# A new order of steps: sums ahead of a hold on GpSimd's queue, and transposes, loads and sums at other places

## The chip, the cores and the metric

The kernel runs on one core of a Trainium2 chip. The time is device time in microseconds (us) of that core. The engines have their own instruction streams and run them in order: TensorE (PE, matmuls and their weight loads), VectorE (DVE), ScalarE (ACT), GpSimd (POOL) and SyncE (SP). DMA transfers are issued from the streams of POOL, SP and ACT. An instruction that waits for a semaphore stops everything behind it in its own stream.

## The reference

Two layers follow each other. The first is an attention without softmax, 8 batches, 8 heads, 576 positions, head size 64:

```
kv  = einsum('bhsd,bhse->bhde', k, v)
out = einsum('bhsd,bhde->bhse', q, kv)
rms = sqrt(mean(out * out, axis=-1, keepdims=True) + 1e-06)
out = out / rms * g_norm
```

Its output, with the heads side by side, is x of shape (8, 576, 512) for the second, a gate with a long convolution:

```
proj = x @ w_proj                       # w_proj: (512, 1536)
x1, x2, x3 = thirds of proj, 512 columns each
X2 = rfft(x2, n=576, axis=1);  H = rfft(filter_fft, n=576, axis=0)
x2_conv = irfft(X2 * H, n=576, axis=1)
y = x1 * x2_conv * x3
return y @ w_out                        # w_out: (512, 512)
```

Inputs and outputs are float32. The kernel multiplies in bfloat16.

## The kernel before

All 8 batches go through one pipeline. A batch is cut into steps, each a Python function of a few instructions on one engine (line numbers are the profile's). The whole program is one string of words, `ORDER` (L20 to L55). A word such as `Ga1.0` means step `Ga1` of batch 0; a third number means that so many filler matmuls (L112) are put in front of it. A loop at the end (L782 to L786) reads the words and calls the steps one after the other:

```
    for word in ORDER.split():
        n, b, *idle = word.split(".")
        b, tmp["idle"] = int(b), int(idle[0]) if idle else 0
        clock[0] += 1
        step[n](b)
```

So the order of the words is the order of the instructions on each engine. Semaphores are set by the framework from what each instruction reads and writes; nothing else decides when something runs. PSUM is four double banks (`ps_0` to `ps_3`, shown as ps_66 to ps_69), handed out by `take` and `free` in the order of the words.

The steps of a batch, in the order in which its data goes through them:

- `Lk`, `Lv`, `Lq` (L140, L144; with a or b: half of the heads) load k, v and q from HBM, issued on POOL's queue and converted to bfloat16 on the way. The buffers kb, vb and qb exist twice, one for even and one for odd batches. `Lw1`, `Lw2`, `Lw3` (L152) load the thirds of w_proj, `Lwo` loads w_out, `Lf` the filter.
- q has to be transposed. For batches 0 and 1 TensorE does it (`T0`, `T1`, L416, copied out by `eTa`, `eTv`). For batches 2 to 7 step `Qt` does it: a DMA transpose from qb to qT, issued on SP's queue (L407), and a copy of two elements of the result on GpSimd (L408, `one__101<-qT`). This copy serves no computation. It waits until the transpose has landed, and since POOL's stream is in order, no later load is issued before that. It is called a hold here.
- `K` (L377) multiplies k by v, `eK` copies the result out, `O` (L447) multiplies by q, `sq`, `ob`, `ov`, `R`, `rs`, `x` (L454 to L489) normalise into x.
- `Ga`, `Gb` (L631) are the gate's matmuls with w_proj's first and third part, `x1`, `xv`, `g` (L637, L639) copy out and multiply the two.
- `eo`, `fa`, `fr` (L501 to L512, VectorE) fold x along the positions, `abM`, `abT`, `rrM`, `rrT` (L529 to L549) multiply with w_proj's second part, `eab`, `eT`, `err` copy out.
- `F0`, `F1t`, `F1`, `F2c`, `F2` (L571 to L598) are the forward transform. Its results in PSUM are multiplied by the filter's spectrum: `M0`, `M1` (L606) write four products in float32 to `tpw`, `M2` (L621) writes to Y directly. These are VectorE instructions with one input in PSUM.
- The products of `M0` and `M1` are added pairwise into Y (L612): `A0`, `A1` on GpSimd, or `Av0`, `Av1` on VectorE.
- `Io`, `I` (L661, L662) are the inverse transform from Y, `oa`, `ea` (L665) copy out, `vB`, `w`, `fin`, `f` (L671 to L683, VectorE, all operands in SBUF) put the pieces together and multiply by the gate.
- `U`, `U4`, `V` (L716, L729, L754) multiply with w_out, `ot`, `va`, `vv` copy out, and DMAs on SP's queue (L723, L736), at the end also on POOL's and ACT's, store the rows.

The steps of neighbouring batches are interleaved, so that the inverse transform of a batch stands among the gates of the next and the attention of the one after. TensorE's stream is in order, too: an inverse transform whose Y isn't complete stops every matmul behind it.

Of the kernel before, what the change touches and what calls it, by code (L numbers as in the profile page):

```python
# [19 lines left out]
ORDER = """Lqa.0 Zi.0 Lva.0 Zd.0 Z.0 T0.0.20 Lka.0 Lvb.0 Zt.0 Lkb.0 An.0 Lqb.0 Zf.0 eTa0.0 Tb2.0.5 Ka.0 eKva.0 Tb0.0 O01.0.3  # L20
sq1.0 Tb1.0.1 sq0.0 ov0.0 Kb.0.4 Lf.0 ob1.0 Lq.1 T1.0.2 eTv1.0 R1.0 Act.0 eKab.0 rs1.0 R0.0.3 O23.0 rs0.0 sq2.0 ob2.0
sq3.0 x0.0 Ff0.0 Lw3.0 ov3.0 Ff1.0 Ff2.0 R3.0 T1.1 rs3.0 T0.1 Lw1.0 R2.0 Lw2.0 eo0.0 rs2.0 x1.0 eTv1.1 eTa0.1 H1.0
eo1.0 H0.0 H2.0 fr.0 Lv.1 Ga1.0 Gb0.0 Lk.1 Lka.2 x11.0 Gb1.0 Ga0.0 fa0.0 fa1.0 Lq.2 rrM.0 HN0.0 g1.0 Lkb.2 x10.0 g0.0
rrT.0 K.1 verr.0 eK.1 Ga3.0 HN1.0 xv3.0 O01.1 sq0.1 F0.0 sq1.1 abM.0 ob1.1 abT.0 M0.0 ob0.1 eab.0 O23.1 eT.0 Lv.2
sq3.1 Lwo.0 F2c.0 ob3.1 F2.0 M2.0 Gb3.0 sq2.1 F1t.0 g3.0 F1.0 Lv.3 R3.1 R2.1 Lq.3 ob2.1 rs3.1 Ga2.0 Qt.2 rs2.1 x12.0
R1.1 K.2 A0.0 M1.0 R0.1 Av1.0 rs1.1 eK.2 Gb2.0 rs0.1 Io01.0 g2.0 oa01.0 Io23.0 oa23.0 I01.0 x.1 ea01.0 O01.2 sq0.2
Lk.3 I23.0 ea23.0 Ga2.1 ob0.2 eo.1 x12.1 Lq.4 fa.1 Ga3.1 sq1.2 x13.1 R0.2 rs0.2 ob1.2 abM.1 vB.0 abT.1 R1.2 eab.1 eT.1
fr.1 rrM.1 Lv.4 O23.2 rs1.2 sq2.2 ob2.2 w.0 F2c.1 rrT.1 fin.0 err.1 F2.1 Gb3.1 sq3.2 F0.1 Lka.4 M2.1 K.3 ob3.2 g3.1
F1t.1 R2.2 Qt.3 Lkb.4 eK.3 M0.1 F1.1 Ga1.1 rs2.2 R3.2 x11.1 Gb2.1 Gb1.1 M1.1 rs3.2 g2.1 O23.3 x1.2 g1.1 x0.2 U0.0 A0.1
sq2.3 sq3.3 eo.2 ob3.3 ob2.3 Ga0.1 fa.2 A1.1 ot0.0 I01.1 Io23.1 ea01.1 x10.1 Gb0.1 I23.1 Io01.1 oa23.1 abT.2 ea23.1  # L30
abM.2 fr0.2 g0.1 fr1.2 oa01.1 O01.3 eT.2 eab.2 Ga1.2 sq1.3 Ga0.2 vB.1 x11.2 R3.3 w.1 ov1.3 x10.2 rs3.3 Lqa.5 K.4 sq0.3
F1t.2 F1.2 Qt.4 rrM.2 fin.1 ob0.3 eKm.4 rrT.2 M1.2 F2c.2 Gb1.2 R0.3 err.2 F2.2 g1.2 rs0.3 F0.2 R1.3 M2.2 Gb0.2 R2.3
rs1.3 U2.0 Lq.6 rs2.3 M0.2 g0.2 Av1.2 Lk.5 ot2.0 x1.3 Ga2.2 x12.2 O23.4 sq2.4 Lv.5 U0.1 A0.2 x0.3 sq3.4 ob3.4 Ga3.2
ot0.1 ob2.4 Gb3.2 eo.3 x13.2 fa.3 I01.2 g3.2 U4.1 fr1.3 ea01.2 I23.2 Io23.2 ea23.2 Lqb.5 Io01.2 oa01.2 abT.3 oa23.2
vB01.2 ot4.1 R2.4 abM.3 eT.3 Gb2.2 vB23.2 rs2.4 eab.3 O01.4 F1t.3 F1.3 fr0.3 g2.2 sq0.4 ob0.4 sq1.4 rrM.3 Lka.6 ob1.4
rrT.3 Ga1.3 M1.3 err.3 x11.3 R1.4 rs1.4 Lkb.6 w023.2 R0.4 F0.3 rs0.4 U2.1 A1.3 Qt.5 ot2.1 w001.2 w123.2 R3.4 Ga0.3
F2c.3 w101.2 f001.2 M0.3 rs3.4 K.5 F2.3 xv0.3 M2.3 f101.2 Gb0.3 Gb1.3 eK.5 f023.2 g0.3 A0.3 Ga2.3 I23.3 I01.3 g1.3
x12.3 Io01.3 ea23.3 f123.2 Qt.6 ea01.3 x0.4 Lv.6 x1.4 Ga3.3 oa01.3 Io23.3 eo.4 x13.3 Gb3.3 O23.5 oa23.3 g3.3 U0.2
sq3.5 ob3.5 sq2.5 Lqa.7 fa.4 ot0.2 abM.4 Gb2.3 ob2.5 O01.5 eab.4 fr.4 g2.3 rrM.4 rrT.4 sq0.5 Lk.7 sq1.5 abT.4 ob1.5
Lqb.7 ob0.5 Ga0.4 R2.5 eT.4 K.6 err.4 F1t.4 F1.4 Lv.7 vB.3 w123.3 x10.4 eK.6 Ga1.4 R3.5 w023.3 rs2.5 w101.3 x11.4  # L40
w001.3 Gb1.4 fin.3 F2c.4 rs3.5 F0.4 M1.4 R1.5 g1.4 U2.2 rs1.5 F2.4 M0.4 Ga3.4 ot2.2 M2.4 x13.4 R0.5 Gb0.4 Av0.4 O23.6
A1.4 rs0.5 sq2.6 Ga2.4 g0.4 sq3.6 Gb2.4 x12.4 x1.5 ov3.6 Io23.4 ob2.6 g2.4 eo1.5 x0.5 I01.4 oa23.4 eo0.5 ea01.4 Qt.7
Io01.4 oa01.4 U4.3 O01.6 ot4.3 fr0.5 fr1.5 sq0.6 I23.4 ea23.4 sq1.6 U0.3 fa.5 vB.4 ob0.6 rrM.5 w.4 ob1.6 R0.6 f001.4
rrT.5 ot0.3 abM.5 Gb3.4 err.5 rs0.6 eab.5 R2.6 F0.5 abT.5 g3.4 R1.6 rs2.6 f101.4 eT.5 f123.4 rs1.6 Ga1.5 K.7 x11.5
F1t.5 eK.7 F2c.5 F2.5 F1.5 Ga0.5 M0.5 M2.5 R3.6 rs3.6 M1.5 U2.3 x10.5 Gb1.5 O23.7 x.6 ot2.3 g1.5 Av0.5 Ga3.5 sq3.7
x13.5 f023.4 Gb3.5 A1.5 Gb0.5 ob3.7 g3.5 sq2.7 Io01.5 oa01.5 Ga2.5 I01.5 g0.5 x12.5 eo.6 ob2.7 Gb2.5 fr.6 Io23.5
oa23.5 ev01.5 Ga3.6 g2.5 fa1.6 I23.5 U0.4 fa0.6 abM.6 ea23.5 xv3.6 ot0.4 vB.5 abT.6 eab.6 eT.6 w.5 O01.7 Ga0.6 F1t.6
sq1.7 F1.6 fin.5 ob1.7 rrM.6 sq0.7 ob0.7 rrT.6 x10.6 F2c.6 F2.6 M1.6 err.6 M2.6 Gb3.6 R0.7 rs0.7 F0.6 g3.6 Ga1.6 R1.7
Gb0.6 x11.6 Gb1.6 rs1.7 M0.6 g0.6 R3.7 R2.7 g1.6 rs3.7 rs2.7 U0.5 Av0.6 A1.6 I01.6 x.7 Io01.6 eo.7 fa.7 Ga2.6 ot0.5
I23.6 ea01.6 oa01.6 fr.7 U2.4 x12.6 Gb2.6 Io23.6 ot2.4 vB01.6 ev23.6 oa23.6 abM.7 eab.7 rrM.7 g2.6 rrT.7 F2c.7 Ga3.7  # L50
abT.7 err.7 F0.7 eT.7 x13.7 vB23.6 w.6 Ga0.7 fin.6 F2.7 F1t.7 x10.7 M0.7 F1.7 M1.7 U0.6 A0.7 M2.7 U2.5 A1.7 Gb0.7
Gb3.7 ot2.5 g0.7 ot0.6 g3.7 I01.7 ea01.7 Io01.7 I23.7 Io23.7 ea23.7 Ga1.7 Gb1.7 ov01.7 oa23.7 x11.7 vB01.7 Ga2.7
vB23.7 w001.7 g1.7 Gb2.7 w023.7 U4.5 x12.7 ot4.5 f001.7 g2.7 w101.7 f023.7 V0a.7 w123.7 f101.7 U4.7 va4.7 f123.7
dg41.7 V0b.7 va0.7 V3.7 dg42.7 U2.6 dg00.7 da02.7 V2.7 V1.7 va3.7 da03.7 da31.7 da01.7 ds43.7 dg30.7 ds40.7 dg32.7
da33.7 va2.7 dg23.7 dg21.7 da22.7 ov2r.6 da20.7 vv1.7 dg13.7 dg11.7 da10.7 da12.7"""  # L55
# [761 lines left out]
```

## Time and profile before

| | |
|---|---|
| median of 3 runs | 234.63 us (234.44 to 237.26) |
| profiled execution | 234.46 us, of which 232.7 us are the profile's span |
| TensorE busy | 205.1 us (88%) |
| VectorE busy | 184.7 us (79%) |
| ScalarE busy | 152.3 us (65%) |
| GpSimd busy | 61.6 us (26%) |
| HBM | 33.69 MB read, 9.44 MB written |

Busy times are unions of the instructions' spans on an engine. Times in the views count from the start of the span. "PEclk" or the granted clock is the share of TensorE's full clock that was granted. In lists of waits, "A <- B" means that A's engine was idle ahead of A until B ended. In the table of windows the columns are, after the window and its length, the busy time and the number of instructions of PE, its weight loads (PEld), DVE, ACT and POOL, then the granted clock, the mean busy share of the DMA engines (it can exceed 1) and GB/s moved.

### The profile page before, as it was taken

What the parts mean: (1) busy time and instruction counts of PE and PEld (TensorE: products, weight loads), DVE (VectorE), ACT (ScalarE), POOL (GpSimd) and SP (SyncE); (2) the same over time, 40 slices, a digit from 0 to 9 for tenths busy, and PEclk for the clock granted to TensorE, in tenths of its full rate; (3) what the DMA queues carried; (4) which work ended last, traced back from release to release, by engine and by line L of the source; (5) the groups of instructions that cost most, each with busy time, mean ns of one, the idle gap of its engine ahead of it and who ended that gap; (6) DMA issues with size and microseconds to landing.
All of it is one profiled execution on the core that took longest, in us unless ns stands there. A gap on an engine that the chain in (4) does not pass through costs nothing.

```text
span 232.7 us, 5024 instructions
## 1 busy us (share of the span) xinstructions
PE 205.1 (88%) x2043; PEld 121.2 (52%) x2043; DVE 184.7 (79%) x271; ACT 152.3 (65%) x238; POOL 61.6 (26%) x72
## 2 busy tenths in 40 slices
...
GB/s 55 176 209 205 207 206 206 195 167 131 152 209 83 37 197 79 207 193 207 115 115 81 180 233 89 191 84 54 35 58 20 73 0 94 90 0 183 59 138 166
DMA packets 37114, 30.16 MB, mean 130 GB/s; under 512 B 16146, under 2 KB 32530, under 8 KB 37090
## 3 DMA queue, kind: packets, MB, share of 16 engines
...
q10 hardware_dynamic: 432, 0.59, 1.0%
q8 instruction: 16, 0.26, 0.4%
q14 instruction: 8, 0.07, 0.1%
HBM read 33.69 MB, written 9.44 MB: 185 GB/s over the span
## 4 chain that ended last, share of the span: by engine, by line
PE 65%; DVE 15%; DMA 7%; ACT 5%; issue 3%; POOL 2%; ACTq 1%; POOLq 0%; DVEq 0%
PE ps L631 19%; DMA qT<-qb 7%; PE ps L716 7%; PE ps L543 6%; PE ps L661 5%; DVE tpw L606 4%; PE ps L112 4%; DVE g L639 3%; PE ps L549 3%; DVE Y L612 2%; PE ps L529 2%; PE ps L447 2%; DVE x L489 2%; PE ps L454 2%; PE ps L377 2%
## 5 line engine op out<-in xcount | busy, mean ns | idle before, releaser
L631 PE MATMUL ps<-x,wp 128*128 128x288 bf16 x512 | 70.6, 286 | 3.0 <-DVE g L639 1.9
L631 PEld LDWEIGHTS <-wp 128*128 128x128 bf16 x512 | 48.8, 98 | 21.4 <-issue 6.9
L612 POOL TENSOR_TENSOR Y<-tpw 128x1024 bf16<-128x1024 f32 (+1 forms) x11 | 27.0, 2459 | 92.1 <-DVE tpw L606 92.1
L606 DVE TENSOR_TENSOR tpw<-ps,HH 97x2048 f32<-97x2048 f32 (+1 forms) x16 | 36.4, 2286 | 2.8 <-PE ps L573 1.0
L468 ACT ACTIVATE rstd<-ps,bias_eps 128x576 bf16<-128x576 f32 x32 | 23.5, 749 | 7.1 <-PE ps L454 7.0
L665 ACT CAST ar<-ps 128x576 bf16<-128x576 f32 x29 | 17.8, 645 | 15.8 <-PE ps L662 15.4
L639 DVE TENSOR_TENSOR g<-ps,x 128x576 bf16<-128x576 f32 x32 | 23.8, 752 | 5.1 <-ACT x L553 2.5
L716 PE MATMUL ps<-wo,yg 128*128 128x512 bf16 x112 | 26.3, 379 | 0.0
L637 ACT CAST x<-ps 128x576 bf16<-128x576 f32 x29 | 18.6, 643 | 9.7 <-PE ps L631 9.6
L662 PE MATMUL ps<-IV,Y 97*128 97x96 bf16 x64 | 13.8, 215 | 11.1 <-POOL Y L612 11.0
L553 ACT CAST x<-ps 128x1024 bf16<-128x1024 f32 (+1 forms) x23 | 19.6, 872 | 6.1 <-PE ps L543 2.4
L457 ACT ACTIVATE sq<-ps 128x576 bf16<-128x576 f32 x32 | 20.4, 656 | 3.0 <-PE ps L447 2.8
L464 ACT ACTIVATE o<-ps,g_col 128x576 bf16<-128x576 f32 x28 | 20.5, 751 | 2.5 <-DVE x L489 2.5
L720 ACT COPY ot<-ps 128x1024 f32<-128x1024 f32 x13 | 13.1, 1015 | 10.3 <-PE ps L716 10.3
L661 PE MATMUL ps<-IV,Y 128*128 128x192 bf16 x128 | 17.2, 257 | 0.0
L716 PEld LDWEIGHTS <-yg 128*128 128x128 bf16 x112 | 10.5, 98 | 11.7 <-issue 0.7
L543 PE MATMUL ps<-wp,ab 128*128 128x512 bf16 x64 | 15.1, 379 | 0.0
L489 DVE TENSOR_TENSOR x<-o,rstd 128x1152 bf16<-128x1152 bf16 (+1 forms) x13 | 13.2, 1031 | 2.2 <-ACT rstd L468 2.1
L671 DVE TENSOR_TENSOR vt<-ar 128x384 bf16<-128x384 bf16 (+1 forms) x11 | 4.9, 443 | 12.1 <-ACT ar L665 12.0
L112 PE MATMUL ps<-nil,ind 128*128 128x512 bf16 x38 | 12.0, 463 | 1.7 <-DVE ind L193 1.6
L621 DVE TENSOR_TENSOR Y<-ps,HM 128x1024 bf16<-128x1024 f32 x8 | 9.8, 1219 | 4.1 <-PE ps L598 2.9
L454 PE MATMUL ps<-sq,ind 128*128 128x288 bf16 x64 | 12.7, 286 | 0.4 <-ACT ff L317 0.4
...
## 6 DMA issues: line engine op xcount, KB each, us to landing
...
vb<-in_v_dram POOLq DMA_DIRECT2D x7, 576.0 KB, 14.0
qb<-in_q_dram POOLq DMA_DIRECT2D x5, 576.0 KB, 13.6
kb<-in_k_dram POOLq DMA_DIRECT2D x8, 288.0 KB, 10.2
kb<-in_k_dram POOLq DMA_DIRECT2D x4, 576.0 KB, 9.5
...
wp<-in_moe_w_proj_dram POOLq DMA_DIRECT2D x3, 512.0 KB, 17.2
...
```

The source lines that it names most:

```text
L112: nc.tensor.matmul(pair[i][:, j], ind, nil, start=True, stop=True)
L457: act.activation(out=halves(sq()[:, j]), in_=tmp['o', b, j][:, :, 0:TH], func=AF.Square)
L464: act.activation(out=halves(osb()[:, j]), in_=i_, func=AF.Copy, scale=g_col)
L468: act.activation(out=halves(rstd()[:, j]), in_=tmp['r', b, j][:, :, 0:TH], func=AF.Abs_reciprocal_sqrt, scale=1.0 / D, bias=bias_eps)
L543: nc.tensor.matmul(pp[:, h], abt()[:, j, 2 * h * P:(2 * h + 1) * P], w2(j), start=(j == 0), stop=(j == NDC - 1))
L553: act.copy(out=o_(), in_=tmp[key, b])
L606: vec.tensor_mul(out=t_[:n], in0=xp[:n].unsqueeze(1).to_broadcast([n, 2, 2, DM]), in1=two)
L612: op(out=Yt()[:n, 2 * g:2 * g + 2], in0=t_[:n, ::-1, 0], in1=t_[:n, ::-1, 1])
L631: nc.tensor.matmul(pp[:, h, 0:TH], w_, x[:, j, h * TH:(h + 1) * TH], start=(j == 0), stop=(j == NDC - 1))
L639: vec.tensor_mul(out=halves(g13t()[:, dc]), in0=pp[:, :, 0:TH], in1=x1)
L661: nc.tensor.matmul(pp[:, i, 0:SB], Y[:, 2 * g + h, cs], IV[:, 2 * g + h, 0:SB], start=(g == 1), stop=(g == 2))
L716: nc.tensor.matmul(pp[:, cc], ygt(b)[:, dc, b % 2 * 64 + c * P:b % 2 * 64 + (c + 1) * P], wo[:, dc], start=(dc == 0), stop=(dc == NDC - 1))
```

## The change

Only the string `ORDER` changes. No step's code is touched, and every batch still goes through the same kinds of steps. What moves, by groups:

- On POOL's queue the sum `A0.0` now stands ahead of the first hold, `Qt.2`, and w_out and batch 3's v are loaded after that hold and not ahead of it. A second hold, `Qt.3`, follows three loads later. Later holds move, too: `Qt.4` and `Qt.5` stand on either side of `A1.2`, and `Qt.7` just ahead of `A0.5`.
- Loads at the start have another order: the first q load is issued after the index patterns (`Zi`), w_proj's parts come as 1, 3, 2 with batch 1's k and v in between, and batch 1's q comes in two halves.
- Which of the 16 sums VectorE does: before `Av1` of batches 0 and 2 and `Av0` of 4, 5 and 6; after `Av1` of 0, 1 and 5 and `Av0` of 2 and 7. GpSimd does the other 11 in both. Batch 1, which had both sums on GpSimd, has now one on each engine.
- Some copies out of PSUM change between ScalarE and VectorE, some wide VectorE steps are split or joined, `U4` is split in halves, and the last output rows are stored in another order. There are 36 filler matmuls where there were 38.

The head of the string and the words around the first hold, cut:

```diff
-ORDER = """Lqa.0 Zi.0 Lva.0 Zd.0 Z.0 T0.0.20 Lka.0 Lvb.0 Zt.0 Lkb.0 An.0 Lqb.0 Zf.0 eTa0.0 Tb2.0.5 Ka.0 eKva.0 Tb0.0 O01.0.3
...
-R1.1 K.2 A0.0 M1.0 R0.1 Av1.0 rs1.1 eK.2 Gb2.0 rs0.1 Io01.0 g2.0 oa01.0 Io23.0 oa23.0 I01.0 x.1 ea01.0 O01.2 sq0.2
+ORDER = """Zi.0 Z.0 Zt.0 Lqa.0 Zd.0 An.0 Zf.0 Act.0 Lva.0 T0.0.22 eTv0.0 Tb1.0 Lka.0 Lvb.0 Tb2.0 Ka.0 eKva.0 Tb0.0 Lqb.0 O01.0.3
...
+Gb0.0 M2.0 g0.0 sq3.1 F1t.0 Lka.2 Lqb.3 Lqa.3 A0.0 Qt.2 F1.0 ob3.1 R1.1 R3.1 Ga2.0 rs1.1 rs3.1 M1.0 R0.1 K.2 x12.0
```

First place: POOL's queue around the first hold, kernel before. Names ending in 70, 72, 74 are the buffers of even batches, 71, 73, 75 those of odd ones; `Y<-tpw` is a sum, `one__101<-qT` a hold.

```order
L140 DMA qb_74<-in_q_dram 96x8x384
L144 DMA kb_70<-in_k_dram 128x2x576
L144 DMA vb_72<-in_v_dram 128x4x576
L152 DMA wo<-in_moe_w_out_dram 128x4x512
L144 DMA vb_73<-in_v_dram 128x4x576
L140 DMA qb_75<-in_q_dram 96x8x384
L408 COPY one__101<-qT 1x2
L612 TENSOR_TENSOR Y<-tpw 97x1024
L144 DMA kb_71<-in_k_dram 128x4x576
```

The same place on POOL's queue in the kernel after, from the load of batch 2's q to the second sum:

```order
L140 DMA qb_74<-in_q_dram 96x8x384
L144 DMA kb_70<-in_k_dram 128x2x576
L140 DMA qb_75<-in_q_dram 96x4x384 x2
L612 TENSOR_TENSOR Y<-tpw 97x1024
L408 COPY one__101<-qT 1x2
L144 DMA kb_71<-in_k_dram 128x4x576
L144 DMA vb_73<-in_v_dram 128x2x576 x2
L152 DMA wo<-in_moe_w_out_dram 128x4x512
L408 COPY one__101<-qT 1x2
L144 DMA kb_70<-in_k_dram 128x4x576
L140 DMA qb_74<-in_q_dram 96x4x384
L140 DMA qb_75<-in_q_dram 96x8x384
```

The first sum and the first hold have changed places, and v of batch 3 and w_out stand behind the hold. The second hold follows on them.

Second place: VectorE's queue at batch 3's products, kernel before. The sum of the first product here (`A1.3`) is GpSimd's.

```order
L606 TENSOR_TENSOR tpw<-ps_66,HH 128x2048
L678 TENSOR_TENSOR w<-bb 128x2x288 x2
L680 TENSOR_TENSOR w<-bb 128x2x288 x2
L683 TENSOR_TENSOR yg<-w,g_108 128x2x288
L606 TENSOR_TENSOR tpw<-ps_69,HH 97x2048
```

The same place in the kernel after:

```order
L606 TENSOR_TENSOR tpw<-ps_67,HH 128x2048
L683 TENSOR_TENSOR yg<-w,g_108 128x4x576
L606 TENSOR_TENSOR tpw<-ps_66,HH 97x2048
L639 TENSOR_TENSOR g_108<-ps_69,x_118 128x576
L621 TENSOR_TENSOR Y<-ps_66,HM 128x1024
```

Five short VectorE instructions on SBUF stood between the two products, and one longer one stands there now; products that read PSUM follow behind it.

68 lines of the change are left out of this document (34 added, 34 removed).

## The prediction

> **What bounds the kernel now.** I read the page's head, the waits by engine, the chain of waits, the timelines of the engines around the longest wait, and then tables of windows.
>
> ```profile
> span 232.7 us, 5024 instructions
> ```
> ```profile
> PE ps L662 <- POOL Y L612: 11.0, 1, 11.0
> PE ps L631 <- DVE g L639: 1.9, 2, 1.0
> PE ps L377 <- DVE tpw L606: 1.7, 1, 1.7
> ...
> PE ps L631 <- ACT o L464: 0.8, 1, 0.8
> ```
>
> The last columns are the total, the number of waits and the longest. TensorE waits for others little, except once: 11.0 us at the inverse transform (L662) for a sum on GpSimd. Windows before, in and behind this stop:
>
> ```profile
> 38.80:50.20 11.40, 8.47 (x130) 4.80 (x128) 9.65 (x9) 8.83 (x15) 0.00 (x0) 1.00 1.27 196
> 50.20:55.60 5.40, 0.00 (x0) 0.00 (x0) 1.53 (x2) 0.00 (x0) 0.00 (x0) 0.60 1.09 120
> 47.30:58.30 11.00, 0.00 (x0) 0.00 (x0) 4.36 (x5) 0.62 (x1) 2.52 (x3) 0.68 1.11 147
> 58.30:61.75 3.45, 3.44 (x30) 2.69 (x31) 0.00 (x0) 2.42 (x4) 3.45 (x6) 0.53 0.81 115
> 61.75:224.40 162.65, 157.07 (x1483) 95.51 (x1480) 145.77 (x185) 113.20 (x176) 36.75 (x30) 1.00 0.58 111
> ...
> 224.40:232.70 8.30, 0.00 (x0) 0.00 (x0) 0.69 (x1) 0.58 (x1) 2.94 (x6) 0.77 0.67 173
> ```
>
> From 47.3 to 58.3 TensorE does nothing, and the next 3.45 us run at a granted clock of 0.53. From 61.75 to its last matmul TensorE is busy 157.07 of 162.65 us: there it is the bound, with VectorE (145.77) close behind. The stop itself, in the chain and then in the timelines of VectorE, GpSimd and TensorE:
>
> ```profile
> 38.84 16.81 DMA qT<-qb
> 55.96 2.31 POOL Y L612
> 58.31 0.26 PE ps L662
> ```
> ```profile
> 37.78 2.29 DVE L606 TENSOR_TENSOR tpw<-ps,HH 97x2048 f32<-97x2048 f32 x1 [0.69 <-DMA qb<-in_q_dram]
> ```
> ```profile
> 55.78 0.17 POOL L408 COPY one__101<-qT 1x2 bf16<-1x2 bf16 x1 [18.72 <-DMA qT<-qb]
> 55.92 2.33 POOL L612 TENSOR_TENSOR Y<-tpw 97x1024 bf16<-97x1024 f32 x1
> ```
> ```profile
> 46.95 0.34 PE L661 MATMUL ps<-IV,Y 128*128 128x192 bf16 x2
> ...
> 60.50 0.69 PE L447 MATMUL ps<-qT,kvblk 64*64 64x288 bf16 x8
> ...
> 61.75 2.12 PE L631 MATMUL ps<-x,wp 128*128 128x288 bf16 x16
> ```
>
> The products of M0.0 were ready at 40.07. GpSimd could have added them by 42.4. It stood in the hold until the transpose of batch 2's q had landed at 55.65. Nothing of the sum depends on this transpose; only the order on the queue does.
>
> **The hold behind the sum.** The new order puts A0.0 first. It is then ready by 42.4 or some us later, and VectorE's own sum of batch 0, behind which the first two matmuls went at 46.95, is the last input. The inverse transform starts at about 47.0, and its 3.45 us at clock 0.53 are 1.8 us at full clock (3.45 x 0.53): it ends at 48.8. What is late next is O01.2, the first step that reads the transposed q; it stands on TensorE behind the inverse transform and ran at 60.50. So the transpose still sets a date. For that I need when it lands now.
>
> ```profile
> 17.40:38.80 21.40, 20.40 (x236) 10.47 (x235) 16.00 (x25) 15.75 (x25) 4.54 (x6) 1.00 1.25 207
> ```
> ```profile
> DMA to landing us min/median/max: 4.7/5.0/16.8
> ```
> ```profile
> kb<-in_k_dram POOLq DMA_DIRECT2D x4, 576.0 KB, 9.5
> ...
> wo<-in_moe_w_out_dram POOLq DMA_DIRECT2D x1, 512.0 KB, 20.4
> ```
>
> The landing times are those of tile qT: a transpose takes 5.0 us from issue to landing, and once 16.8. That one was issued while loads were moving. Loads ran at 196 to 207 GB/s until about 50.2; then 5.4 us at 120 GB/s followed, which is about a lone transpose. I read this as: it got nearly nothing until the loads had drained. Before, all loads up to batch 3's q were on the queue ahead of the hold. Now the same are, without w_out (512 KB) and v of batch 3 (as large as a k, 576 KB): 1.11 MB at 206 GB/s are 5.4 us. The loads drain at 44.8, the transpose lands at about 49.9, O01.2 ends 0.4 us later, and the gates that began at 61.75 begin at 50.4. **Gain 11.3 us.** If the transpose were no limit, it would be 12.6 (gates at 49.2); if it lands 3 us later, 8.
>
> The Trainium skill (DMA: Bandwidth & Descriptors, "Queues, rings and completion order") says that each DMA engine serves its queues in turn, a packet at a time. By that rule the transpose of 0.59 MB would have had half of 206 GB/s beside the loads and landed 5.7 us after its issue at 38.84; the trace's 16.81 us disagree. By that rule the transpose would come in time and the gain would be the 12.6 us.
>
> **The start.** w_proj's second part moves behind k and v of batch 1:
>
> ```profile
> 10.27 0.74 POOL L152 DMA_DIRECT2D wp<-in_moe_w_proj_dram  x1 [0.47 <-DMA kb<-in_k_dram]
> ```
> ```profile
> DMA to landing us min/median/max: 15.4/17.2/18.4
> ```
> ```profile
> 32.23 1.04 PE L529 MATMUL ps<-wp,rr 128*128 128x512 bf16 x4
> ```
>
> Issued at 10.27, this part landed at about 27.5 (17.2 is tile wp's median) and was used at 32.23. The 1.18 MB more ahead of it are 5.7 us: 33.2. In front of its use TensorE now has two gates that came later before (16 matmuls, 2.1 us in the row at 61.75) and K.1, so it gets there at 34.3 or later. The cover is 1.1 us; if it is gone, TensorE stops for what is missing. The activation table load moves ahead of ScalarE's busy stretch, and the first q load behind three short index instructions; the two point in opposite ways at a start that loads limit. Together 0, between -1 and +1.5.
>
> **Sums beside products.** Beside some sums VectorE was slow:
>
> ```profile
> L612 DVE TENSOR_TENSOR Y<-tpw x5: 1212/1225/3004, 45.7 to 190.7; 97x1024 bf16<-97x1024 f32 x3, 128x1024 bf16<-128x1024 f32 x2
> ```
> ```profile
> L489 DVE TENSOR_TENSOR x<-o,rstd x13: 742/752/2602, 18.7 to 191.8; 128x1152 bf16<-128x1152 bf16 x10, 128x2304 bf16<-128x2304 bf16 x3
> ```
> ```profile
> 76.45 2.60 DVE L489 TENSOR_TENSOR x<-o,rstd 128x1152 bf16<-128x1152 bf16 x1
> ...
> 97.91 3.00 DVE L612 TENSOR_TENSOR Y<-tpw 128x1024 bf16<-128x1024 f32 x1
> ...
> 113.69 2.97 DVE L678 TENSOR_TENSOR w<-bb 128x576 bf16<-128x576 bf16 x2
> ...
> 167.83 2.71 DVE L612 TENSOR_TENSOR Y<-tpw 97x1024 bf16<-97x1024 f32 x1
> ```
> ```profile
> 73.76 4.67 POOL L612 TENSOR_TENSOR Y<-tpw 97x1024 bf16<-97x1024 f32 x2 [11.70 <-DVE tpw L606]
> ...
> 97.48 2.35 POOL L612 TENSOR_TENSOR Y<-tpw 97x1024 bf16<-97x1024 f32 x1 [6.36 <-DVE tpw L606]
> ...
> 113.86 2.48 POOL L612 TENSOR_TENSOR Y<-tpw 128x1024 bf16<-128x1024 f32 x1 [11.96 <-DVE tpw L606]
> ...
> 166.06 3.40 POOL L612 TENSOR_TENSOR Y<-tpw 128x1024 bf16<-128x1024 f32 x1 [13.85 <-DVE tpw L606]
> ```
> ```profile
> L606 DVE TENSOR_TENSOR tpw<-ps,HH x16: 2276/2291/2292, 37.8 to 205.7; 97x2048 f32<-97x2048 f32 x8, 128x2048 f32<-128x2048 f32 x8
> ```
>
> Four VectorE instructions or pairs with both inputs in SBUF took 2.6 to 3.0 us with a sum beside them; the smallest and median of the same lines say 0.75 for L489 and 1.21 for L612. They lost 1.9, 1.8, 1.5 and about 2 us, 7.2 together. The products, with one input in PSUM, never left 2.28 to 2.29. What the end sees of it are TensorE's waits of 1.9 + 1.7 + 0.8 = 4.4 us: these lie right behind the four places, elsewhere TensorE was busy.
>
> The new order doesn't free all sums. Behind the products whose sums go to GpSimd, VectorE's next instruction reads PSUM for A0.0, A0.1, A1.2, A0.3, A1.4, A0.6 and A1.7, but for A1.3, A1.6 and A0.5 it is L683 from SBUF, and A0.4 follows A1.4 and meets an L489. That are four places again, as many as were slow. But at 166.06 the L489 in front was whole and GpSimd was slow instead (3.40 for 2.36), so a long L683 that starts together with the sum may cost nothing. I take **-2 us** of the 4.4, between -4.4 and 0.
>
> The Trainium skill (SBUF — State Buffer, "Who interferes with whom") says that a VectorE instruction with two SBUF inputs and a GpSimd instruction that reads SBUF exclude each other, the one that issues first for its whole length. By that rule up to four times 2.36 us would be lost again, and this term would be 0.
>
> **New waits and the end.** In a new order other waits appear which no row of before shows; from 61.75 on, TensorE was idle 5.6 us, 1.2 without the three above. Below, it can't be under -1.2. Above I bound it by the largest of these waits coming up three times, +5.1. I take **+1**, near what is there now. The end:
>
> ```profile
> 224.43 0.69 DVE L760 COPY kb<-ps 128x512 f32<-128x512 f32 x1 [0.50 <-PE ps L754]
> ...
> 225.66 0.58 ACT L760 COPY vb<-ps 128x512 f32<-128x512 f32 x1 [1.51 <-DMA out_dram<-kb]
> ```
>
> The last two copies out of PSUM lay 1.2 us apart because the second waited for ScalarE's DMA queue; now both are VectorE's and can follow 0.7 us apart. **-0.7** with what else moves there, between -1.5 and +1.
>
> Sum: -11.3 - 2 + 1 - 0.7 = -13.0 us against the profiled execution: its span of 232.7 becomes 219.7, and with the 1.76 us that lie around the span in this execution (234.46 in all, close to the median 234.63) **221.5 us**.
>
> **The rivals.**
>
> *The stop moves to O01.2.* If the transpose needs its 16.8 us from the landing of q whatever else moves, it lands late again. q of batch 2 had landed at 38.84 and has 0.59 MB more ahead of it: 41.7 + 16.8 = 58.5, and the gates begin at 58.9 for 61.75. Gain 2.9, with the other terms 4.6: 230. For it speaks that there is only one slow transpose, against it that its last 5.4 us look like a whole lone one.
>
> *The exclusion bites as often as before.* The second term is 0: 223.5. For it speak the four places above, against it the 3.40 us row.
>
> *The new order has its own stops*, with VectorE at 146 of 163 us leaving little slack: 5 to 10 us of the 13 are lost, 226 to 231.
>
> *Slower: the moved holds.* Qt.4 now stands directly ahead of A1.2 and Qt.7 directly ahead of A0.5, and both have loads on POOL's queue shortly ahead of them. The new Qt.3 has k, v and w_out moving beside it and A0.1 behind it. A lone transpose lands in 5.0 us and these sums wait 0 to 2 us, which is in my +1. If all three take 16.8 us, each sum is 11.8 us later than behind a lone one. The four sums quoted above found GpSimd idle for 6.4 to 13.9 us; with loads and a hold in that time I estimate 5 us of slack. 3 x 6.8 = 20.4 us, less the 13.0 of gain: 242. It turns to slower from about 9 us of lateness at each. Against it: the median of the six transposes is 5.0 us.
>
> **How the numbers follow.** Forecast 0.55, exclusion 0.15, stop at O01.2 0.12, own stops 0.11, slower 0.07. The forecast's own range is 217.5 to 226.5 from the bounds above: 11.3 between 8 and 12.6, the second term between -4.4 and 0. To hold 8 in 10 the range goes up into the own stops and near the moved stop, to 229.5. A change of 2% is 4.7 us, about what a measurement of this kernel can tell: faster is below 229.9. That takes in the first two, most of the own stops and a little less than half of the moved stop: 0.82, which I round to 0.80; slower than 239.3: 0.06; the rest 0.14.
>
> **What would show it.** Right: GpSimd's sum of batch 0 ends ahead of its hold, TensorE's wait for L612 at the first inverse transform is gone, O01.2 runs at about 50, the granted clock stays 1.00 there, and the transpose of batch 2 lands near 50. The second term shows in the largest durations of L489, L612 and L678. Wrong: a TensorE wait of over 3 us at L447 for qT or at L661 and L662 for a later sum behind a hold, or a stop for loads before 47.

## The result, and the profile after

The changed kernel takes 220.5 us, the median of 4 runs (220.25 to 221.13), beside 234.82 us for the kernel before on the same chip. The ratio is 0.936, with a 95% interval of 0.929 to 0.943: 14.3 us less. The forecast was 221.5 us in a range of 217.5 to 229.5. The time is right; three of the four stretches that it is added up from are not, and the experiments below are about all four. Two of the 39 runs of the kernel before, of 297.58 and 238.0 us, were slow executions and are left out of every comparison here.

The profiled execution took 221.13 us. Head of its page:

```profile
span 219.3 us, 4987 instructions
...
PE 200.9 (92%) x2017; PEld 120.7 (55%) x2041; DVE 184.4 (84%) x284; ACT 146.8 (67%) x227; POOL 66.0 (30%) x72
```

The span fell by 13.4 us, from 232.7. The engines are busy about as long as before; what went is mostly time in which TensorE stood still. Its waits now:

```profile
PE ps L112 <- DVE ind L193: 1.6, 1, 1.6
PE ps L662 <- DVE Y L612: 1.4, 1, 1.4
```

The 11.0 us behind GpSimd's sum are gone, and behind the start the longest wait is 1.4 us, for one of VectorE's own sums. The place of the old stop, in the timelines of GpSimd, of SP's queue and of TensorE:

```profile
43.12 2.36 POOL L612 TENSOR_TENSOR Y<-tpw 97x1024 bf16<-97x1024 f32 x1 [6.00 <-DVE tpw L606]
48.31 0.79 POOL L408 COPY one__101<-qT 1x2 bf16<-1x2 bf16 x1 [2.83 <-DMA qT<-qb]
```
```profile
41.76 7.37 SPq L407 DMA_TRANSPOSE qT<-qb  x2
```
```profile
49.12 0.34 PE L661 MATMUL ps<-IV,Y 128*128 128x192 bf16 x2
...
51.28 0.44 PE L447 MATMUL ps<-qT,kvblk 64*64 64x288 bf16 x8
51.85 2.12 PE L631 MATMUL ps<-x,wp 128*128 128x288 bf16 x16
```

The sum (43.12) now ends ahead of the hold (48.31). O01.2 (L447) follows the inverse transform at 51.28 without a wait, and the next gates begin at 51.85, where they began at 61.75. The four stretches by which the prediction had cut the time, in the table of windows of the kernel after:

```profile
0.00:49.12 49.12, 44.29 (x525) 22.98 (x530) 38.31 (x86) 31.13 (x48) 18.95 (x32) 0.97 1.13 184
49.12:51.85 2.73, 2.52 (x33) 2.01 (x33) 2.73 (x4) 2.68 (x7) 2.73 (x4) 1.00 0.94 134
51.85:209.17 157.32, 154.04 (x1461) 95.74 (x1479) 141.50 (x193) 112.41 (x174) 41.34 (x32) 1.00 0.63 120
209.17:219.30 10.13, 0.00 (x0) 0.00 (x0) 1.89 (x3) 0.54 (x1) 2.95 (x6) 0.67 0.64 181
```

| stretch | before | after | change | predicted |
|---|---|---|---|---|
| start, to the first inverse matmul | 46.95 | 49.12 | +2.2 | 0 |
| the stop, from there to the next gates | 14.80 | 2.73 | -12.1 | -11.3 |
| steady part, to TensorE's last matmul | 162.65 | 157.32 | -5.3 | -2 + 1 |
| behind the last matmul | 8.30 | 10.13 | +1.8 | -0.7 |
| span | 232.7 | 219.3 | -13.4 | -13.0 |

And the operations that had been slow beside a sum, all runs of each line in the kernel after (smallest, median and largest duration in ns, after the count):

```profile
L612 DVE TENSOR_TENSOR Y<-tpw x5: 1212/1217/1292, 47.8 to 194.3; 128x1024 bf16<-128x1024 f32 x3, 97x1024 bf16<-97x1024 f32 x2
L612 POOL TENSOR_TENSOR Y<-tpw x11: 2347/2362/3462, 43.1 to 192.1; 97x1024 bf16<-97x1024 f32 x6, 128x1024 bf16<-128x1024 f32 x5
L678 DVE TENSOR_TENSOR w<-bb x11: 446/457/757, 56.6 to 203.9; 128x576 bf16<-128x576 bf16 x6, 128x1152 bf16<-128x1152 bf16 x5
L489 DVE TENSOR_TENSOR x<-o,rstd x12: 747/754/1546, 22.7 to 178.0; 128x1152 bf16<-128x1152 bf16 x8, 128x2304 bf16<-128x2304 bf16 x4
```

On VectorE little is slow any more: the largest value of L678 is that of its wide form, and two L489 take 0.2 and 0.5 us more than their forms usually do (at 129.29 and 176.76). GpSimd's sums bear what is left: three of them take 3.40 to 3.46 us for 2.36.

### The profile page after: what moved, and what is told of

Its sections match the earlier page's. It is cut to its first block, busy times and chain, and to the rows that moved or that the text cites. A ratio compares the mean times of both kernels' runs of the same rounds, so it can differ in the third digit from the quotient of the medians.

```text
span 219.3 us, 4987 instructions
## 1 busy us (share of the span) xinstructions
PE 200.9 (92%) x2017; PEld 120.7 (55%) x2041; DVE 184.4 (84%) x284; ACT 146.8 (67%) x227; POOL 66.0 (30%) x72
## 4 chain that ended last, share of the span: by engine, by line
PE 79%; DVE 6%; ACT 5%; issue 4%; POOL 2%; POOLq 0%; DVEq 0%; ACTq 0%
PE ps L631 27%; PE ps L716 11%; PE ps L543 6%; PE ps L661 4%; PE ps L454 4%; PE ps L529 3%; PE ps L549 3%; PE ps L377 2%; PE ps L447 2%; PE ps L536 2%; PE ps L587 2%; PE ps L573 2%; POOL out_dram L765 2%; PE ps L332 1%; PE ps L112 1%
## 5 line engine op out<-in xcount | busy, mean ns | idle before, releaser
L612 POOL TENSOR_TENSOR Y<-tpw 97x1024 bf16<-97x1024 f32 (+1 forms) x11 | 29.1, 2648 | 64.4 <-DVE tpw L606 64.3
L553 ACT CAST x<-ps 128x1024 bf16<-128x1024 f32 (+1 forms) x21 | 18.6, 893 | 8.4 <-PE ps L543 4.7
L720 ACT COPY ot<-ps 128x1024 f32<-128x1024 f32 x14 | 14.2, 1017 | 13.8 <-PE ps L716 12.1
L637 ACT CAST x<-ps 128x576 bf16<-128x576 f32 x27 | 17.5, 647 | 7.5 <-PE ps L631 5.6
L464 ACT ACTIVATE o<-ps,g_col 128x576 bf16<-128x576 f32 x25 | 18.7, 753 | 0.0
L408 POOL COPY one__101<-qT 1x2 bf16<-1x2 bf16 x6 | 4.0, 670 | 46.7 <-DMA qT<-qb 46.7
L716 PEld LDWEIGHTS <-yg 128*128 128x128 bf16 x112 | 10.8, 98 | 12.3 <-issue 0.9
L661 PE MATMUL ps<-IV,Y 128*128 128x192 bf16 x128 | 15.9, 245 | 0.1
L662 PE MATMUL ps<-IV,Y 97*128 97x96 bf16 x64 | 13.2, 207 | 1.4 <-DVE Y L612 1.4
L140 POOL DMA_DIRECT2D qb<-in_q_dram x12 | 8.9, 745 | 12.6 <-PE ps L416 9.9
L112 PE MATMUL ps<-nil,ind 128*128 128x512 bf16 x34 | 10.7, 441 | 2.0 <-DVE ind L193 1.6
L489 DVE TENSOR_TENSOR x<-o,rstd 128x1152 bf16<-128x1152 bf16 (+1 forms) x12 | 11.9, 1008 | 0.6 <-ACT rstd L468 0.6
```

The lines of the kernel that those rows point to most:

```text
L464: act.activation(out=halves(osb()[:, j]), in_=i_, func=AF.Copy, scale=g_col)
L553: act.copy(out=o_(), in_=tmp[key, b])
L612: op(out=Yt()[:n, 2 * g:2 * g + 2], in0=t_[:n, ::-1, 0], in1=t_[:n, ::-1, 1])
L661: nc.tensor.matmul(pp[:, i, 0:SB], Y[:, 2 * g + h, cs], IV[:, 2 * g + h, 0:SB], start=(g == 1), stop=(g == 2))
L716: nc.tensor.matmul(pp[:, cc], ygt(b)[:, dc, b % 2 * 64 + c * P:b % 2 * 64 + (c + 1) * P], wo[:, dc], start=(dc == 0), stop=(dc == NDC - 1))
```

## The experiments

Only words of the order are changed in all of them, and none leaves out work. They ran in three sets of four, each beside its own runs of the kernel before: medians 235.14 us for x1 to x4, 236.39 for x5, x6, x7 and x10, and 234.86 for x8, x11, x12 and x13.

### The stop: x1_sum_first and x2_sum_and_loads

Kernel before, first the sum alone, then the loads as well:

```diff
 x1:
-Ga2.0 Qt.2 rs2.1 x12.0 R1.1 K.2 A0.0 M1.0
+Ga2.0 A0.0 Qt.2 rs2.1 x12.0 R1.1 K.2 M1.0
 x2, besides:
-sq3.1 Lwo.0 F2c.0 ... F1.0 Lv.3 R3.1 ... A0.0 Qt.2 rs2.1
+sq3.1 F2c.0 ... F1.0 R3.1 ... A0.0 Qt.2 Lv.3 Lwo.0 rs2.1
```

> The kernel before, with one edit: the sum A0.0 stands ahead of the hold Qt.2; no load is moved. Theory (the sum's place and the loads each hold a part of the 11 us): the inverse transform starts at about 47 and ends at 48.8, but the transpose still lands at 55.65 as before, because the same loads move beside it; TensorE then waits for it at O01.2 (L447), some 6 us, and the gates (L631) begin at about 57 for 61.75: 4.8 us less, about 230 us. Rival 1 (the sum's place is all of it): gates at about 50, 223 us. Rival 2 (the inverse transform waited for something else): no wait goes, 234.6 us.

> As x1_sum_first, and w_out and v of batch 3 (1.11 MB) are loaded behind the hold Qt.2 in place of ahead of it; nothing else is changed against the kernel before. Theory: the transpose lands about 5.4 us earlier, near 50, and O01.2 waits for little: gates at 50 to 51, some 11 us less than before, 223 to 224 us. Rival 1 (the transpose takes 16.8 us from its issue whatever moves beside it): as x1_sum_first, 230 us. Rival 2 (loads have nothing to do with it and x1_sum_first gives all): no difference between the two.

x1 took 232.2 us (ratio 0.984, 0.978 to 0.990), x2 226.48 us (0.960, 0.953 to 0.967). TensorE's wait and the gates in x1, then in x2:

```profile
PE ps L447 <- DMA qT<-qb: 6.9, 1, 6.9
```
```profile
56.61 3.48 PE L631 MATMUL ps<-x,wp 128*128 128x288 bf16 x16
```
```profile
PE ps L377 <- DMA kb<-in_k_dram: 2.7, 1, 2.7
PE ps L447 <- DMA qT<-qb: 1.8, 1, 1.8
```
```profile
50.98 2.12 PE L631 MATMUL ps<-x,wp 128*128 128x288 bf16 x16
```

The stop moves as the theory had it. With the sum ahead of the hold the stop moves to O01.2 (L447), and the gates begin at 56.61, where 57 was expected. Taking the loads away brings the transpose forward and the gates to 50.98, where 50 to 51 were expected. Both times are 2 to 3.5 us longer than expected, for reasons of their own: in x1 the gates behind the stop run at a low clock (3.48 us for 2.12) and the granted clock falls to 0.50 once more, from 117.4 to 120.8, and in x2 the loads that stand behind the hold are late for K.3 (L377), 2.7 us. That price of moving loads had not been thought of.

The five microseconds ahead of 50, x1 first and x2 second (the last two columns are the DMA engines' busy share and GB/s):

```profile
45.00:50.00 5.00, 3.35 (x92) 2.60 (x79) 4.63 (x6) 4.28 (x9) 0.00 (x0) 1.00 1.43 187
```
```profile
45.00:50.00 5.00, 3.38 (x96) 2.63 (x83) 4.63 (x6) 4.31 (x9) 0.00 (x0) 1.00 1.13 142
```

In x1 DMA moves 187 GB/s in this stretch, and the transpose lands at 55.2. In x2 most of the loads ahead of it are through by then: the rate is 142 GB/s, and L447 runs at 50.18. So 1.11 MB of loads cost the transpose 5.0 us; 5.4 were predicted.

### The same two, taken back from the kernel after: x3_hold_first and x4_loads_first

```diff
 x3:
-Lqb.3 Lqa.3 A0.0 Qt.2 F1.0
+Lqb.3 Lqa.3 Qt.2 A0.0 F1.0
 x4:
-Lqb.3 Lqa.3 A0.0 Qt.2 F1.0 ... Io01.0 Lva.3 ea01.0 eo.1 I23.0 Lvb.3 O01.2 Lwo.0 oa01.0
+Lqb.3 Lqa.3 Lva.3 Lvb.3 Lwo.0 A0.0 Qt.2 F1.0 ... Io01.0 ea01.0 eo.1 I23.0 O01.2 oa01.0
```

> The kernel after, with one edit: the hold Qt.2 stands ahead of the sum A0.0 again, as in the kernel before; the loads stay where they are. Theory: the transpose lands at 48.1 as in the kernel after, the hold ends at about 48.4, the sum 2.36 us later at 50.8, and the inverse transform starts at about 51 for 49.12: 1.5 to 2.5 us more than the kernel after, 222 to 223 us. Rival (the order of sum and hold on the queue is worth 11 us by itself): 231 us.

> The kernel after, with one edit: v of batch 3 and w_out are loaded ahead of A0.0 and Qt.2 again; the sum stays ahead of the hold. Theory (a transpose gets next to nothing until the loads issued ahead of it have drained): it lands 5.4 us later, near 53.5, O01.2 waits some 2.3 us for it: 222 to 223.5 us. Rival 1 (transpose and loads share the DMA engines evenly): it lands by 50 and nothing is lost, 220.5 us. Rival 2 (it takes 16.8 us as in the kernel before): it lands at 58.5, O01.2 waits 7 us, 227 to 228 us.

x3 took 226.83 us and x4 227.49: 6.3 and 7.0 us more than the kernel after, both well over the 1.5 to 3 us that the theories gave. In x3 the waits of TensorE, the hold and the sum, and the stretch behind the stop:

```profile
PE ps L662 <- POOL Y L612: 4.7, 1, 4.7
```
```profile
50.42 0.26 POOL L408 COPY one__101<-qT 1x2 bf16<-1x2 bf16 x1 [14.42 <-DMA qT<-qb]
50.64 2.33 POOL L612 TENSOR_TENSOR Y<-tpw 97x1024 bf16<-97x1024 f32 x1
```
```profile
53.00:57.00 4.00, 3.97 (x34) 3.03 (x35) 2.11 (x5) 3.02 (x5) 4.00 (x7) 0.57 0.70 93
```

And in x4 the wait and the gates:

```profile
PE ps L447 <- DMA qT<-qb: 5.4, 1, 5.4
```
```profile
56.03 3.70 PE L631 MATMUL ps<-x,wp 128*128 128x288 bf16 x16
```

The waits are where they were expected, but longer, and then the clock falls. In x4 the transpose lands at 55.35 (issued at 41.88, 13.5 us), not at 53.5; x4's time lies where the rival that gives a transpose 16.8 us had it, but the landing doesn't: its 58.5 is 3 us later. In x3 the transpose lands at 50.3, and not at 48.3 as in the profiled execution of the kernel after with the same loads ahead of it. There the kernel after is the odd one: in x7, x8, x10, x12 and x13, which have these loads too, it lands between 49.9 and 50.3. Against those five, x4 lands about 5.3 us later, close to the 5.4 that 1.11 MB were expected to cost. Why one execution had it 2 us earlier isn't settled. Behind the stop TensorE works at a granted clock of 0.57 for 4 us in x3, and in x4 the gates take 3.70 us for 2.12: some 1.6 us more in addition to each wait.

Together: the sum's place alone gives 2.9 us (x1), with the loads 8.7 (x2), both against their own kernel before; from the kernel after, taking back either one costs 6.3 or 7.0. Neither edit is the gain by itself, because each leaves TensorE waiting for the same transpose, through the sum or through O01.2.

How the loads hold the transpose up shows in the packets of the two queues. These are the kernel before from 43 to 50 us, while the transpose waits to land; q0 are the loads, and q1 is here the transpose alone (packets, MB, share of the 16 engines):

```profile
q0 software_dynamic: 1064, 1.05, 91.7%
q1 hardware_dynamic: 1049, 0.27, 31.8%
```

The transpose isn't kept waiting until the loads are through, as the prediction and the expectation of x4 had it. It moves from 43 on, one packet for one packet of the loads (in x4, from 46 to 50, 609 beside 606). But 0.27 MB in 1049 packets are about 260 bytes each, and a packet of the loads holds about 990, so the transpose gets 38 GB/s beside their 150. In the stretch from 50.2 to 55.6 that the prediction took for a lone transpose, loads still moved; the lone transpose comes next, from 56 to 59:

```profile
q0 software_dynamic: 460, 0.34, 47.6%
```
```profile
q1 hardware_dynamic: 2240, 0.57, 100.8%
```

The Trainium skill (DMA: Bandwidth & Descriptors, "Queues, rings and completion order") has each DMA engine serve its queues in turn, packet by packet. The counts agree with it. What disagrees is the share that the prediction worked out from it: half of the packets were a fifth of the bytes, and with half of the bytes the transpose of x4 would have landed 5.7 us after its issue and not 13.5.

### The sums beside VectorE: x5_sums, x6_rebuild, x11_mended

A meeting is a sum on GpSimd beside a VectorE instruction on SBUF that slows one of the two. x5 was to take the four slow meetings out of the kernel before; x6 puts x2 and x5 together and loads k first; x11 mends two waits of x6:

```diff
 x5:
-Ga0.1 fa.2 A1.1 ot0.0
+Ga0.1 fa.2 Av1.1 ot0.0
-M1.2 F2c.2 ... g0.2 Av1.2 Lk.5 ... U0.1 A0.2 x0.3
+M1.2 A1.2 F2c.2 ... g0.2 Av0.2 Lk.5 ... U0.1 x0.3
-U2.1 A1.3 Qt.5
+U2.1 Av1.3 Qt.5
-M0.4 Ga3.4 ... Gb0.4 Av0.4 O23.6 A1.4 rs0.5
+M0.4 A0.4 Ga3.4 ... Gb0.4 Av1.4 O23.6 rs0.5
 x6 (x2 and x5), besides:
-A0.0 Qt.2 Lv.3 Lwo.0
+A0.0 Qt.2 Lk.3 Lv.3 Lwo.0
 x11 (x6), besides:
-M2.1 K.3 ob3.2 ... Lkb.4 eK.3 M0.1 ... R3.2 x11.1 Gb2.1 Gb1.1
+M2.1 ob3.2 ... Lkb.4 M0.1 ... R3.2 K.3 x11.1 Gb2.1 eK.3 Gb1.1
-x0.2 U0.0 A0.1 ... fa.2 Av1.1 ot0.0
+x0.2 U0.0 Av1.1 A0.1 ... fa.2 ot0.0
```

> The kernel before, with the four slow meetings of a sum and a VectorE instruction on SBUF taken out and nothing else: batch 1's second sum and batch 3's second sum go to VectorE; in batches 2 and 4 GpSimd's and VectorE's sum change places, so that GpSimd's starts while VectorE reads PSUM. GpSimd then has 9 sums for 11. Theory: the four VectorE instructions or pairs that took 2.6 to 3.0 us come back to 0.75 to 1.5, and of TensorE's 4.4 us of waits behind them (for L639's g, L606's tpw, L464's o) 3 to 4.4 go: 230 to 231.5 us; two sums more on VectorE cost it 2.4 us, which TensorE doesn't see. Rival 1 (the waits are made of something else, or VectorE's two sums more cost as much): 234 to 235 us. Rival 2 (the steady part gains what it gained between the two kernels): 3.5 us, 231 us.

> The kernel before with x2_sum_and_loads and x5_sums together, and the load of batch 3's k directly behind the first hold, ahead of v and w_out, because K.3 (L377) waited 2.7 us for it in x2_sum_and_loads. Theory (the stop, the load of k and the sums are separate and add up): 226.5 - 2.7 - 3.5, about 220.5 us, as the kernel after, with some ten words of the order changed. Rival 1 (the sums give nothing): 223.8 us. Rival 2 (the new order's gain comes from its other moves): 225 us or more.

> x6_rebuild with two of its waits mended: K.3 with its copy stands some steps later on TensorE (it waited 2.2 + 0.5 us for batch 3's loads), and VectorE's own sum of batch 1 stands ahead of batch 2's folding (TensorE waited 2.3 us for it, a wait that x5_sums had made). Theory (the sums' meetings did cost TensorE 2.8 us, and x5_sums lost them again by its own misplaced sum): both waits go, 226.7 - 2.7 - 2.3, about 221.7 us; 2.3 us of it are what x5_sums should have gained. Rival 1 (the meetings don't matter; other waits of the same length take the places): 225 to 227 us. Rival 2 (only the loads' wait is real): 224 us.

x5 gained nothing: 237.17 us, ratio 1.005 (1.001 to 1.010). In that set the kernel before itself ran between 234.1 and 237.5 us, at a mean clock between 0.971 and 0.955, so half a per cent of x5 is not to be read. TensorE's waits in x5:

```profile
PE ps L661 <- DVE Y L612: 2.5, 1, 2.5
PE ps L631 <- DVE g L639: 1.6, 2, 0.8
...
PE ps L377 <- DVE tpw L606: 0.7, 1, 0.7
```

The wait for tpw fell from 1.7 to 0.7, the 0.8 us for L464's o are gone, and those for g went from 1.9 to 1.6. But the edit had made a wait of its own: VectorE's sum of batch 1 stood behind the folding of batch 2, and the inverse transform waited 2.5 us for it. x6 (226.73 us) inherited that, and the wait of x2 at K.3, too: with k loaded first it is v that comes late.

```profile
PE ps L661 <- DVE Y L612: 2.3, 1, 2.3
PE ps L377 <- DMA vb<-in_v_dram: 2.2, 1, 2.2
```

Both expectations were missed in part through edits that made waits. x11 takes these two away, and its time is the one expected: 221.54 us (0.943, 0.937 to 0.948). From the gates to the last matmul, x11 needs

```profile
49.25:211.13 161.88, 155.86 (x1461) 95.40 (x1479) 146.56 (x190) 113.61 (x176) 37.68 (x35) 1.00 0.64 123
```

161.88 us, 0.8 less than the kernel before (162.65); the rest of x11's gain over x6 is the two waits that x6 had added. But the edit of x5 doesn't take out all four meetings, and x6 and x11 have it, too. It changes the sums of batches 1 to 4, and the fourth slow meeting, at 167.83 in the kernel before, is that of batch 5 (A1.5 and Av0.5). In batch 4, where none had been slow, it makes a new one. VectorE's sums of batches 4 and 5 in x11:

```profile
130.87 2.47 DVE L612 TENSOR_TENSOR Y<-tpw 128x1024 bf16<-128x1024 f32 x1
```
```profile
154.57 2.71 DVE L612 TENSOR_TENSOR Y<-tpw 97x1024 bf16<-97x1024 f32 x1
```

With one L683 of 1.43 us for 0.45, at 107.27, VectorE still loses 3.7 us in x11, where it had lost 7.2. So x11 doesn't show what the four meetings cost: with half of VectorE's loss gone, the steady part is 0.8 us shorter. TensorE's waits for g and tpw are still 1.6 and 0.7 us there, for 1.9 and 1.7, and the one for o (0.8) is gone.

### One meeting put back into the kernel after: x10_short_fin

```diff
-F0.3 M1.3 fin.2 A1.3 ot2.1
+F0.3 M1.3 f001.2 f101.2 f023.2 f123.2 A1.3 ot2.1
```

> The kernel after; in batch 2 the product with the gate (L683), one VectorE instruction of 128x2304 beside which the sum A1.3 runs, is cut into four of 128x576. Theory (whichever of the two engines has started first keeps the other out until its instruction ends): the sum gets in behind the first of the four, one of the others takes about 2.3 us more for 0.45, the sum itself takes 2.4 us for 3.4, and 0 to 2 us of it reach the end: 220.5 to 222.5 us. Rival (VectorE goes first anyway, or the two run side by side): four times 0.45 us, 220.5 us.

It took 222.78 us; x7_filler, which ran beside it and has nothing changed there, 220.36. In x10 the four short products in VectorE's line, the sum, and the wait of TensorE:

```profile
L683 DVE TENSOR_TENSOR yg<-w,g x20: 445/454/2618, 56.7 to 206.8; 128x576 bf16<-128x576 bf16 x16, 128x2304 bf16<-128x2304 bf16 x4
```
```profile
102.85 2.50 POOL L612 TENSOR_TENSOR Y<-tpw 128x1024 bf16<-128x1024 f32 x1 [12.43 <-DVE tpw L606]
```
```profile
PE ps L594 <- DVE tpw L606: 1.9, 1, 1.9
```

In the kernel after, the same place reads:

```profile
104.09 1.35 DVE L683 TENSOR_TENSOR yg<-w,g 128x2304 bf16<-128x2304 bf16 x1
105.36 2.29 DVE L606 TENSOR_TENSOR tpw<-ps,HH 97x2048 f32<-97x2048 f32 x1
```
```profile
104.27 3.40 POOL L612 TENSOR_TENSOR Y<-tpw 128x1024 bf16<-128x1024 f32 x1 [12.48 <-DVE tpw L606]
```

With one long instruction, GpSimd's sum waits until VectorE has finished and then runs beside the next product, which reads PSUM: 3.40 us for 2.36, and VectorE loses nothing. With four short ones the sum gets in behind the first and takes its usual time, and one of the others takes 2.62 us for 0.45. The next product is late by that, TensorE waits 1.9 us for it, and the kernel is 2.4 us slower. This is the rule of the Trainium skill (SBUF — State Buffer, "Who interferes with whom"): of a VectorE instruction with two SBUF inputs and a GpSimd instruction that reads SBUF, the one that issues first keeps the other out for its whole length. The trace agrees in both directions.

### The start: x7_filler

```diff
-eTv0.0 Tb1.0 Lka.0
+eTv0.0 Tb1.0.5 Lka.0
```

> The kernel after, with five filler matmuls (1.9 us) at Tb1.0, where TensorE stands still for 1.1 us at 8.4 to 9.5 and the granted clock is 0.50 a little later, 0.83 over 10 to 20. Theory (the low clock is most of what the start lost): the clock stays at 1.00, the first inverse matmul (L661) starts 1 to 2 us earlier than at 49.12, about 219 us. Rival (the start is set by loads, VectorE and ScalarE, or the difference at the start is only this one profiled execution's): 220 to 221 us.

220.36 us (220.0 to 220.62): the rival. The stretch 10 to 20 of x7, and of the kernel after:

```profile
10.00:20.00 10.00, 9.66 (x150) 5.02 (x149) 6.55 (x18) 7.41 (x12) 4.29 (x7) 1.00 1.20 207
```
```profile
10.00:20.00 10.00, 9.60 (x139) 5.13 (x142) 6.04 (x17) 7.07 (x12) 4.09 (x7) 0.83 1.20 206
```

The clock is back at 1.00, and the first inverse matmul starts at 48.25. But it started between 47.7 and 48.1 also in x3, x4, x8, x10, x12 and x13, which have the start of the kernel after without this filler, and in all six at a clock of 1.00 over the same stretch. The profiled execution of the kernel after had a start some 1.2 us longer than that start usually takes. DMA moved 206 to 207 GB/s in either.

### The end: x8_tail_queues, x12_own_sum, x13_both

In the kernel after SP's queue and ScalarE's at the end read:

```profile
200.56 11.25 SPq L736 DMA_DIRECT2D out_dram<-ot  x4
```
```profile
206.42 2.53 ACTq L765 DMA_DIRECT2D out_dram<-sq  x2
209.12 0.59 ACT L760 COPY vb<-ps 128x512 f32<-128x512 f32 x1 [2.73 <-DMA out_dram<-sq]
```

The first of the four L736 stores was issued at 200.56, the second at 209.63; DMA moved almost nothing between 202 and 206. What SP's queue waited for:

```profile
SPq L736 <- DMA out_dram<-sq: 9.0, 2, 8.7
```

The stores of `sq` are on ScalarE's queue and on GpSimd's. In the trace SP's and ScalarE's stores use eight completion semaphores in turn, and each waits for the store that had its semaphore before. SP's second store has that of ScalarE's first, which was issued at 206.42 and landed at 209.62. The edits (ten stores change their queue in x8, not 13 as its expectation says):

```diff
 x8 (issuing queue: a = ScalarE, g = GpSimd, s = SP):
-V0.7 da42.7 da40.7 ... da32.7 ... da33.7 da00.7 ... da02.7 ... dg12.7 dg10.7 dg22.7 da20.7 da21.7
+V0.7 ds42.7 ds40.7 ... dg32.7 ... dg33.7 dg00.7 ... dg02.7 ... ds12.7 ds10.7 dg22.7 ds20.7 dg21.7
 x12:
-ov4r.1 Gb2.2 Av0.2 I01.2
+Av0.2 ov4r.1 Gb2.2 I01.2
```

> The kernel after; the last stores of batch 7 that ScalarE's queue issued are issued by SP and GpSimd instead (13 moved by one queue or another, none of the copies). In the kernel after SP's queue issues one store at 200.56 and the next at 209.63, although the data of all seven that come next were copied out by 205.9, and ScalarE's last copy stands behind its own two stores until 209.12. Theory (stores of SP's and of ScalarE's queue take eight semaphores in turn, and a store waits for the one that had its semaphore before, so SP's wait for ScalarE's): without stores on ScalarE's queue SP issues the seven by 208, ScalarE's copy starts at about 207.5 for 209.12, VectorE's behind it too, and the end comes 2.5 to 4 us earlier: 216.5 to 218 us. Rival 1 (the end is set by the rate at which the stores' bytes go out): 220 to 220.5 us. Rival 2 (GpSimd's eleven stores of 0.5 us each become the last): 220 to 222 us.

> The kernel after; VectorE's own sum Av0.2 stands one VectorE instruction earlier, ahead of the copy L733 that waits 2.3 us, so that TensorE's largest wait of the steady part (1.4 us at L662 for this sum) goes. Theory (TensorE is the bound there): 1 to 1.4 us less, about 219.3 us. Rival (the copy, now later, frees its PSUM later and TensorE waits for that): 220.5 us or more.

> The kernel after with the edits of x8_tail_queues and of x12_own_sum. Theory (they lie in different parts and add up): 215 to 217 us. Rival (the end doesn't follow TensorE): as the better of the two.

| kernel | us | ratio to the kernel before | 95% interval |
|---|---|---|---|
| after | 220.5 | 0.936 | 0.929 to 0.943 |
| x8_tail_queues | 217.35 | 0.924 | 0.920 to 0.929 |
| x12_own_sum | 218.93 | 0.931 | 0.927 to 0.935 |
| x13_both | 216.45 | 0.920 | 0.915 to 0.925 |

The end of x8, SP's queue, ScalarE and the window of the end:

```profile
199.38 2.59 SPq L736 DMA_DIRECT2D out_dram<-ot  x4
```
```profile
206.30 0.59 ACT L760 COPY vb<-ps 128x512 f32<-128x512 f32 x1 [1.09 <-PE ps L754]
```
```profile
207.99:215.60 7.61, 0.00 (x0) 0.00 (x0) 1.29 (x2) 0.00 (x0) 3.82 (x8) 0.69 0.60 170
```

SP issues the four L736 in 2.59 us, the copy waits only for its matmuls, and the stretch behind the last matmul is 7.61 us for 10.13: 2.5 us less. In x12 the wait of 1.4 us at L662 is gone and the steady part is 156.21 us long for 157.32: 1.1 us less. x13 has both, and its median lies 4.1 us under that of the kernel after; it is the fastest kernel of the study.

## Why the prediction was right, point by point

**The stop.** Right in place and size: -12.1 us for -11.3. x1 to x4 show its steps one by one: the sum waits for nothing but the order, O01.2 comes next, and loads ahead of the transpose hold it up. The forecast had the transpose land at 49.9 and the gates begin at 50.4. In the profiled execution it landed at 48.3 and TensorE, which reached the inverse transform late, never waited for it; in x7, x8, x10, x12 and x13, with the same loads ahead, it landed at 49.9 to 50.3, O01.2 began within 0.3 us of it, and the gates began at 50.5 to 51.0. One step of the mechanism is wrong: the transpose was taken to get next to nothing until the loads had drained, and then to run alone for 5.4 us at 120 GB/s. It had 0.27 MB of its 0.59 through by 50 in the kernel before, loads moved 0.34 MB in those 5.4 us, and alone it moved 0.57 MB in 3 us. That the date came out all the same is luck in part. What the forecast also missed is a price of moved loads: K.3 waits 2.7 us for them in x2. The kernel after doesn't pay it; no run changed the place of K.3 in that kernel, so that this is due to its later place there is argued, not shown.

**The start.** The term 0, between -1 and +1.5, was mis-sized: +2.2 in the profiled execution. About 1.0 of it is the order (47.7 to 48.1 in six kernels with this start, 46.6 to 47.2 in six with the old one), within the bounds that were given. The rest belongs to this one execution. Which change of the order costs the 1.0 wasn't tried. One new wait of TensorE stands in all the traces with this start and in none with the old one, 0.7 us at L598 (at 43.17 in the kernel after) for ScalarE's copy L553; it isn't a wait for a load.

**Sums beside products.** The mechanism stands: x10 shows it in both directions, and the largest durations on VectorE fell as foreseen. The step that failed is the size, -2 "of the 4.4": none of the waits that make up the 4.4 is left in the kernel after. The term was halved because four places were kept. At three of these the two met, but it was GpSimd's sum that took longer (3.40, 3.46 and 3.40 us), as the 3.40 us row had suggested, and VectorE lost about 0.7 us in all and not up to four times 2.36. One meeting the other way round costs 2.4 us at the end (x10). What the four of the kernel before had cost there stays open, since x11 takes away only half of VectorE's loss.

**New waits, +1.** The largest that came is the 1.4 us at L662, worth 1.1 us in the steady part (x12). With two smaller ones they are 1.9 us, 1.0 more than what was there beside the 4.4 before (0.7 at L754 and 0.2). Right.

**The steady part as a whole** was under-sized: -5.3 for -1. TensorE's named waits behind the stop were 5.3 us before (1.9 + 1.7 + 0.8 + 0.7 + 0.2) and are 1.9 now (1.4 + 0.3 + 0.2), 3.4 less: -4.4 and +1.0. The other 1.9 us of the 5.3 are not settled. TensorE's busy time there is 3.0 us less (157.07 to 154.04) for the same matmuls at the same granted clock, but it can't be compared: records are missing in the trace of the kernel after, 3 of 7 at L598 and 2 of 7 in one form of L587, and the holes that they leave count as idle. x11 lacks the same ones.

**The end, -0.7.** Wrong in sign: +1.8. The prediction saw the two last copies move to VectorE, and didn't follow the stores on ScalarE's queue (nine in the old order, eight in the new): in the new order SP's stores wait for the first of them, and ScalarE's last copy stands behind two, 2.5 us in all (x8).

**The sum** came out at -13.0 for -13.4 because +2.2 at the start and +2.5 at the end, against what was put there, met -4.3 in the steady part and -0.8 in the stop. That the time came within 1.0 us is partly luck, as these errors are of opposite sign.

**The rivals.** The moved stop at O01.2 didn't come: it takes a transpose that is slow whatever moves, and x2 and x4 show that it depends on the loads. It does come with loads ahead (x1, x4). The exclusion did bite, at three of the four places foreseen, but on GpSimd, where TensorE didn't wait for it. Stops of the new order's own were at most 1.4 us. The slower case, three late holds, was far off. The landing times of qT in the kernel after:

```profile
DMA to landing us min/median/max: 4.8/6.3/6.8
```
